# Attention plus gated dense branch: an ordering flag for VectorE at the last softmax sums, two PSUM banks for each first projection, and one load on another queue

## The chip, the core and the metric

The kernel runs on one NeuronCore of a Trainium2 chip. The core has TensorE (PE in the profile; its weight loads are PEld), VectorE (DVE), ScalarE (ACT), GpSimd (POOL) and SyncE (SP). DMAs are issued here from SP's queue and from ScalarE's queue. PSUM has eight banks, numbered 0 to 7 in this text; one bank holds 512 fp32 values in each of 128 partitions. The metric is the device time of one execution in microseconds; lower is better.

## The reference

Two branches are computed from the same input and mixed by a gate for each row. Branch A is attention with 32 heads of 20 columns each, over 2048 positions; branch B is a dense layer with a Mish activation.

```python
# x: (1, 2048, 640)   wqkv: (640, 1920)   wo: (640, 640)   w1: (640, 1536)   w2: (1536, 640)
g = sigmoid((x * gate_w).sum(-1, keepdims=True))

qkv = (x @ wqkv).reshape(B, S, 3, H, Dh).transpose(2, 0, 3, 1, 4)     # H = 32, Dh = 20
q, k, v = qkv[0], qkv[1], qkv[2]
p = softmax(einsum("bhqd,bhkd->bhqk", q, k) * Dh ** -0.5)
o = einsum("bhqk,bhkd->bhqd", p, v)
a = o.transpose(0, 2, 1, 3).reshape(B, S, D) @ wo

h = x @ w1 + b1
b = (h * tanh(softplus(h))) @ w2

out = g * a + (1 - g) * b
```

## The kernel before

**Tiling.** The 32 heads are taken four at a time, so there are 8 head groups p; the 2048 queries are taken in 4 chunks of 512. One pair (p, chunk) is a group, and there are 32 of them. In each, the scores of 16 key tiles are made for four heads, exponentiated (ScalarE on L1312, or a power-of-two approximation on VectorE on L473, L604 and GpSimd on L572) and multiplied with the values into the accumulator `acc`, which is PSUM bank 7 (L1355). A column of ones in the value tile gives the softmax sums beside the products.

**Order.** The order of the instructions on each engine is written out by hand: a small planner in the kernel's Python steps through a model of four engines and emits instructions as its model's engines come free. Each engine then runs its own stream in that order and waits on semaphores for the others. The planner takes VectorE's work from the list `dve_q`; an item carries a priority as its first field, and the lowest due time wins (`step_dve`). Items of priority 0 are the ones of `normalise`, below. Everything else on VectorE has priority 1 or more: evacuations of PSUM, powers, scalings.

**Start.** The first 512 rows of x come in four pieces (L317), two on each of the queues of SP and ScalarE. Then come the first columns of the K weights (`wf1`, `load_first(1)`, SP), the first columns of the Q weights (`wf0`, `load_first(0)`, ScalarE), `w_top` (48 further columns of the K weights, which go into the unused columns of the padded tile; L320, SP) and `wv0` (value weights of the first four heads; L321, ScalarE; the profile calls it `wv`). Behind them SP issues the rest of x and all other weights. The four pieces of x are transposed on TensorE (L1454) into `xT`. VectorE copies `wf1` and `w_top` into the padded tile `wkp` (L366, L1469) and `wf0` into `wqp` (L366). Then five products of 512 columns make the first K in one bank and five make the first Q in another (L1478). Of each result VectorE copies the first 256 columns (L1486) and ScalarE the last 256 (L1487), out of the same bank. The first scores (L1262) need both halves of both.

**End.** The last group is (p = 7, chunk 3). `normalise` handles it with four steps at priority 0, each put into the list when the one before is done: `a` transposes the accumulator (L1376), `b` takes the reciprocal of the sums and multiplies it by the gate (L1390, L1392), and `ends` scales and transposes the result in two halves (L1413, L1419) into `o_last[7]`. Heads groups 0 to 5 of the last chunk go through the output projection in eight chains of 16 products each (`wo_chain`, L637); each is evacuated on VectorE by L1064 into `R[LQ]` (in the tile `big`), for one 128-row block u and one half of the columns. After the planner's loop, 24 products fill all eight banks (`rest`, L1830): eight with `o_last[6]`, eight that add `R[LQ]` through the identity, eight with `o_last[7]`, always in the order u = 0 to 3, first half and second half. The banks by that order are 0, 1, 3, 4, 2, 5, 6, 7. Then the blocks are copied out and stored: blocks 0 and 1 on ScalarE, 128x640 each (L1845), both halves of block 2 and the first half of block 3 on VectorE (L1854), and the second half of block 3 on ScalarE (L1852). SP stores each block when it is ready (L1848, L1856).

Of the kernel before, what the change touches and what calls it, by code (L numbers as in the profile page):

```python
# [9 lines left out]
P = 128  # L10
# [54 lines left out]
def kernel(  # L65
# [12 lines left out]
    nc = tc.nc  # L78
    _, S, D = A_x.shape
    F = B_w1.shape[1]  # L80
    H = 32
    DH = D // H
    KT = D // P
    FT = F // P
    NS = S // P
    QC = 512
# [3 lines left out]
    HALF = D // 2  # L90
# [149 lines left out]
    xT = consts.tile([P, KT, S], BF16, tag="xT")  # L240
    VA = consts.tile([P, NS, H, DH + 1], BF16, tag="VA")
    wv0 = work.tile([P, KT, 4 * DH + 1], BF16, tag="bl1", name="wv0")
# [7 lines left out]
    wqp = consts.tile([P, KT, 4, 32], BF16, tag="wqp")  # L250
    wkp = consts.tile([P, KT, 4, 32], BF16, tag="wkp")
# [4 lines left out]
    allb = psum.tile([P, 8, QC], F32, tag="Sp", name="Sp")  # L256
# [3 lines left out]
    def bank_ap(tag, shape, dtype=F32):  # L260
        ap = allb[:, tag, :]
        if dtype != F32:
            ap = ap.bitcast(dtype)
        if len(shape) == 3:
            return ap[:, 0 : shape[1] * shape[2]].rearrange("p (a b) -> p a b", b=shape[2])
        return ap[:, 0 : shape[1]]
# [9 lines left out]
    wrows = A_wqkv.rearrange("(kt p) c -> p kt c", p=P)  # L276
# [8 lines left out]
    KTOP = D - KPAD  # L285
# [9 lines left out]
    w_top = work.tile([P, KT, KPAD], BF16, tag="bl0", name="w_top")  # L295

    def load_first(kind, eng):
        eng.dma_start(out=w_first[kind][:, :, :], in_=wrows[:, :, kind * D : kind * D + HF])
# [16 lines left out]
    for u in range(NU):  # L315
        eng = nc.sync if u % 2 == 0 else nc.scalar
        eng.dma_start(out=xs[0][:, u, :], in_=x2d[u * P : (u + 1) * P, :])  # L317
    load_first(1, nc.sync)
    load_first(0, nc.scalar)
    nc.sync.dma_start(out=w_top[:, :, :], in_=wrows[:, :, D + KTOP : 2 * D])  # L320
    nc.scalar.dma_start(out=wv0[:, :, 0 : 4 * DH], in_=wrows[:, :, 2 * D : 2 * D + 4 * DH])  # L321

    def load_x(c):
        nc.sync.dma_start(
# [6 lines left out]
        out=wv0[:, :, 4 * DH : 4 * DH + 1], in_=gate_w.rearrange("(kt p o) -> p kt o", p=P, o=1)  # L331
# [58 lines left out]
    act_q = deque()  # L390
    pool_q = []
    two_port = [0.0]
    seq = [0]
    free = {"PE": 0.0, "ACT": 0.0, "DVE": 0.0, "POOL": 0.0}
    mode = [None]
# [973 lines left out]
    def normalise(G, ready):  # L1369
        p, qc = groups[G]  # L1370
        i = G % 2
        st = {}

        def a(t):
            st["T1"] = work.tile([P, NS, 32], F32, tag=f"T1_{i}", name="T1")
            nc.vector.transpose(out=st["T1"][:, :, :].rearrange("p b r -> p (b r)"), in_=acc[:, :])  # L1376

        pr = 0 if G == NG - 1 else 2
        kept = qc == LQ and p >= NQ - NSB

        def a_done(t):
            acc_free[0] = t
            if G == NG - 1:
                dve(t, t, 140.0, b, prio=pr, done=lambda t: dve(t, t, 1300.0, ends, prio=pr))
                return
            dve(t, t, 140.0, b, prio=pr, done=lambda t: pool_q.insert(0, (t, 728.0, c, c_done, None)))

        def b(t):
            st["rec"] = work.tile([P, NS], F32, tag=f"rec{i}", name="rec")
            nc.vector.reciprocal(out=st["rec"][:, :], in_=st["T1"][:, :, DH])  # L1390
            if kept:
                nc.vector.tensor_tensor(  # L1392
                    out=st["rec"][:, :], in0=st["rec"][:, :], in1=g_rows[:, :], op=ALU.mult
                )

        def c(t):
            nc.gpsimd.tensor_tensor(  # L1397
                out=T2[i][:, :].rearrange("p (b r) -> p b r", r=32)[:, :, 0:DH],
                in0=st["T1"][:, :, 0:DH],
                in1=st["rec"][:, :].unsqueeze(2).to_broadcast([P, NS, DH]),  # L1400
                op=ALU.mult,
            )

        def d(t):
            st["O"] = work.tile([P, QC], BF16, tag=f"O{i}", name="O")
            nc.vector.transpose(out=st["O"][:, :], in_=T2[i][:, :])

        def ends(t):
            st["O"] = work.tile([P, QC], BF16, tag=f"O{i}", name="O")
            for h in range(2):  # L1410
                q = slice(h * QC // 2, (h + 1) * QC // 2)
                b_ = slice(h * NS // 2, (h + 1) * NS // 2)
                nc.vector.tensor_tensor(  # L1413
                    out=T2[i][:, q].rearrange("p (b r) -> p b r", r=32)[:, :, 0:DH],
                    in0=st["T1"][:, b_, 0:DH],
                    in1=st["rec"][:, b_].unsqueeze(2).to_broadcast([P, NS // 2, DH]),
                    op=ALU.mult,
                )
                nc.vector.transpose(out=st["O"][:, q], in_=T2[i][:, q])  # L1419
            o_last[p] = st["O"]  # L1420

        def c_done(t):
            if kept:
                dve(t, t, 640.0, d, prio=pr, done=lambda t: o_last.__setitem__(p, st["O"]))
                return
            rows = o_dram[qc * QC : (qc + 1) * QC, :].rearrange("(b i) f -> i b f", i=32)
            for k in range(4):
                r0 = (4 * p + k) * DH
                nc.sync.dma_start(
                    out=rows[:, :, r0 : r0 + DH],  # L1430
                    in_=T2[i][32 * k : 32 * k + 32, :].rearrange(
                        "p (b r) -> p b r", r=32
                    )[:, :, 0:DH],
                )
            last_p = NQ - 1 - (NSB if qc == LQ else 0)
            early = last_p * HF // P
            if p == last_p - 1 and qc != LQ:
                load_o(qc, range(early))
            elif p == last_p:
                load_o(qc, range(early, -(-(p + 1) * HF // P)))  # L1440
                o_ready[qc] = t + 9000.0
                if qc == LQ - 1:
                    load_o(LQ, range((NQ - NSB - 1) * HF // P))

        dve(0.0, ready, 640.0, a, prio=0, done=a_done)
# [24 lines left out]
        out=wkp[:, :, :, DH:32], in_=w_top[:, :, :].rearrange("p k (h d) -> p k h d", h=4)  # L1470
    )
    pad_copy(nc.vector, wqp, w_first[0][:, :, :])
    sb = [bank_ap(g, [P, QC]) for g in (6, 2)]
    kT[0] = kTb[0]
    qT[0] = qTb[0]
    for w, dst, k in ((wkp, kT[0][:, 0:QC], 0), (wqp, qT[0][:, :], 1)):
        for kt in range(KT):
            nc.tensor.matmul(  # L1478
                sb[k][:, :],
                lhsT=w[:, kt, :, :].rearrange("p h d -> p (h d)"),  # L1480
                rhs=xT[:, kt, 0:QC],
                start=(kt == 0),
                stop=(kt == KT - 1),
            )
        h_ = QC // 2
        nc.vector.tensor_copy(out=dst[:, 0:h_], in_=sb[k][:, 0:h_])  # L1486
        nc.scalar.copy(out=dst[:, h_:QC], in_=sb[k][:, h_:QC])  # L1487
    for p in range(NQ - NSB, NQ):
        tag = "wqp" if p < NQ - 1 else f"wo{p}"
        wo_pad[p] = consts.tile([P, D], BF16, tag=tag, name=f"wo{p}")  # L1490
# [249 lines left out]
    def step_dve(t):  # L1740
        best = None
        for it in dve_q:
            if it[1] <= t and (it[6] is None or it[6](t)):
                due = it[1] + (WAIT0, rule.WAIT1, rule.WAIT2, MWAIT)[it[0]]
                if it[0] == 3:
                    due = min(due, it[7] + WAIT3)
                if it[6] is not None and it[0] == 2 and cur["G"] > pv_G[0]:
                    due = min(due, it[1] + rule.WAITU)
                rank = (due, it[2])
                if best is None or rank < best[0]:  # L1750
                    best = (rank, it)
        if best is None:
            return None
        best = best[1]
        dve_q.remove(best)
        _, _, _, cost, fn, done, _, _ = best
        if rule.MERGE and best[2] in powers:
            o = beside(best, t)
            if o:
                dve_q.remove(o)  # L1760
                both(best, o, t)
                cost = 1134.0
                for x in (best, o):
                    x[5](t + cost + DVE_TAIL + SEM)
                return cost
        if best[0] == 2 and best[6] is not None:
            cost += max(free["POOL"] - t, 0.0)
            two_port[0] = t + cost
        fn(t)
        if done:  # L1770
            done(t + cost + DVE_TAIL + SEM)
        return cost
# [71 lines left out]
    for u in range(2):  # L1844
# [1 line left out]
            out=ots_[u][:, :].rearrange("p (a c) -> p a c", a=2), in_=(tx, ty)[u][:, 0:2, 0:HALF]  # L1846
        )
        nc.sync.dma_start(out=rows_[u], in_=ots_[u][:, :])  # L1848
    for u, half, eng in ((2, 0, 0), (2, 1, 0), (3, 0, 0), (3, 1, 1)):
        dst, src = ots_[u][:, half * HALF : (half + 1) * HALF], places[u][half][:, 0:HALF]  # L1850
        if eng:
            nc.scalar.copy(out=dst, in_=src)  # L1852
        else:
            nc.vector.tensor_copy(out=dst, in_=src)  # L1854
        if half:
            nc.sync.dma_start(out=rows_[u], in_=ots_[u][:, :])  # L1856
    if DEBUG:
        print("model end us", t / 1e3, "last exp", last_exp[0] / 1e3, {k: v / 1e3 for k, v in idle.items()}, "sets", sum(n_d), n_d, "heats", heats[0])

# [29 lines left out]
```

## Time and profile before

| | us |
|---|---|
| median of three runs | 722.08 |
| lowest and highest of them | 721.22, 722.51 |
| the profiled execution, its own time | 722.37 |
| span of the profiled execution, first to last instruction | 720.6 |
| TensorE busy in the span | 704.9 (98%) |
| ScalarE busy | 700.0 (97%) |
| VectorE busy | 631.6 (88%) |
| GpSimd busy | 418.1 (58%) |
| mean granted TensorE clock | 0.995 |

The span is 1.8 us shorter than the execution's time; that difference lies around the instructions. The profile lists the instructions of each engine with their lines in the kernel, the idle time before them and what ended it. "Chain of waits" stands for the view that follows the work that ended last back to what released it. Busy time of TensorE is modelled from pipelined products, so 98% is not 98% of its peak.

### The profile page before, as it was taken

What the parts mean: (1) busy time and instruction counts of PE and PEld (TensorE: products, weight loads), DVE (VectorE), ACT (ScalarE), POOL (GpSimd) and SP (SyncE); (2) the same over time, 40 slices, a digit from 0 to 9 for tenths busy, and PEclk for the clock granted to TensorE, in tenths of its full rate; (3) what the DMA queues carried; (4) which work ended last, traced back from release to release, by engine and by line L of the source; (5) the groups of instructions that cost most, each with busy time, mean ns of one, the idle gap of its engine ahead of it and who ended that gap; (6) DMA issues with size and microseconds to landing.
All of it is one profiled execution on the core that took longest, in us unless ns stands there. A gap on an engine that the chain in (4) does not pass through costs nothing.

```text
span 720.6 us, 24680 instructions
## 1 busy us (share of the span) xinstructions
PE 704.9 (98%) x10262; PEld 230.7 (32%) x10262; DVE 631.6 (88%) x1062; ACT 700.0 (97%) x726; POOL 418.1 (58%) x669
## 2 busy tenths in 40 slices
PE   7999999999999999999999999999989999999997
PEld 3433332222222333333333222222223333333333
DVE  4499998968868889999999998999998989999996
ACT  6899999999999999999999999999989999999996
POOL 2002864557868776877676687867964486762000
PEclk9999999999999999999999999999989999999999
DMA  9611122132322211111230223212211131131301
GB/s 249 180 24 33 31 47 52 34 69 57 80 43 51 50 29 17 23 32 28 46 92 25 46 51 84 65 43 43 60 20 30 33 68 27 31 63 15 61 20 47
DMA packets 123312, 37.86 MB, mean 53 GB/s; under 512 B 90880, under 2 KB 122640, under 8 KB 123200
## 3 DMA queue, kind: packets, MB, share of 16 engines
q1 hardware_dynamic: 121600, 35.76, 22.8%
q8 instruction: 80, 1.31, 0.8%
q10 hardware_dynamic: 1600, 0.53, 0.3%
q14 instruction: 32, 0.26, 0.2%
HBM read 22.29 MB, written 11.48 MB: 47 GB/s over the span
## 4 chain that ended last, share of the span: by engine, by line
PE 66%; ACT 25%; issue 5%; DVE 2%; DMA 1%; SPq 0%; POOL 0%; DVEq 0%; ACTq 0%
ACT E L1312 24%; PE Sp L1262 23%; PE Sp L637 21%; PE Sp L1355 21%; DVE T L473 1%; ACT big L924 1%; DMA w_top<-in_A_wqkv_dram 1%; PE Sp L1830 0%; DMA qT<-q_dram 0%; PE Sp L1478 0%; DVE T L604 0%; DMA q_dram<-st 0%; ACT L1312 0%; ACT L924 0%; DVE st L741 0%
## 5 line engine op out<-in xcount | busy, mean ns | idle before, releaser
L1312 ACT ACTIVATE E<-Sp 128x1024 bf16<-128x1024 f32 x710 | 668.8, 1079 | 6.8 <-PE Sp L1262 6.4
L572 POOL TENSOR_TENSOR T<-T,step_t 128x256 int32<-128x256 int32 x624 | 389.3, 659 | 108.0 <-PE Sp L1355 83.4
L473 DVE TENSOR_SCALAR T<-Sp 128x512 int16<-128x512 f32 (+1 forms) x595 | 391.9, 686 | 52.4 <-PE Sp L1262 46.3
L1262 PE MATMUL Sp<-qT,kT 32*128 32x512 bf16 x2048 | 288.3, 385 | 6.4 <-ACT E L1312 1.8
L1262 PEld LDWEIGHTS <-kT 32*128 32x128 bf16 x2048 | 74.2, 91 | 264.2 <-issue 260.0
L1355 PE MATMUL Sp<-E,VA 128*21 128x512 bf16 x1448 | 138.2, 383 | 0.0
L1397 POOL TENSOR_TENSOR T<-T,rec 128x320 bf16<-128x320 f32 x31 | 24.6, 792 | 164.9 <-DVE rec L1390 140.8
L604 DVE TENSOR_SCALAR T<-T 128x2048 int16<-128x2048 int16 x144 | 117.2, 819 | 1.4 <-PE Sp L1355 0.4
L1355 PE MATMUL Sp<-T,VD 128*21 128x512 bf16 x1200 | 113.5, 383 | 1.3 <-DVE T L604 1.3
L637 PE MATMUL Sp<-w_sb,big 128*32 128x320 bf16 x1536 | 79.4, 306 | 0.0
L637 PE MATMUL Sp<-xT,w1t 128*32 128x512 bf16 x960 | 76.6, 383 | 0.0
L1355 PEld LDWEIGHTS <-VA 128*21 128x21 bf16 x2048 | 45.2, 90 | 74.9 <-issue 67.3
L1355 PE MATMUL Sp<-T,VA 128*21 128x512 bf16 x600 | 58.2, 384 | 0.0
L637 PE MATMUL Sp<-xT,ws 128*32 128x512 bf16 x720 | 54.8, 382 | 0.2 <-DVE T L473 0.2
L637 PEld LDWEIGHTS <-big 128*32 128x32 bf16 x1536 | 34.8, 96 | 28.1 <-issue 18.5
L1355 PEld LDWEIGHTS <-VD 128*21 128x21 bf16 x1200 | 28.9, 90 | 37.5 <-issue 32.7
L891 DVE TENSOR_SCALAR big<-Sp,b1f 128x512 bf16<-128x512 f32 x48 | 35.6, 741 | 0.5 <-PE Sp L637 0.2
L637 PE MATMUL Sp<-wv,xT 128*32 128x81 bf16 (+2 forms) x960 | 33.0, 258 | 1.0 <-DVE T L473 1.0
L637 PE MATMUL Sp<-wo_sb,od 128*32 128x320 bf16 (+1 forms) x608 | 32.6, 302 | 0.0
L637 PEld LDWEIGHTS <-w1t 128*32 128x32 bf16 x960 | 19.6, 94 | 26.3 <-issue 21.2
L741 DVE CAST st<-Sp 128x512 bf16<-128x512 f32 x36 | 24.4, 681 | 3.8 <-PE Sp L637 3.3
L1376 DVE STREAM_TRANSPOSE T<-Sp 128x512 f32<-128x512 f32 x32 | 22.7, 709 | 2.1 <-PE Sp L1355 1.8
(74 smaller groups left out, 198.2 us busy)
## 6 DMA issues: line engine op xcount, KB each, us to landing
w1t<-in_B_w_dram SPq DMA_DIRECT2D x24, 320.0 KB
q_dram<-st SPq DMA_DIRECT2D x20, 128.0 KB
out_dram<-ot SPq DMA_DIRECT2D x16, 160.0 KB
qT<-q_dram SPq DMA_DIRECT2D x124, 20.0 KB
o_dram<-T SPq DMA_DIRECT2D x120, 20.0 KB
kT<-k_dram SPq DMA_DIRECT2D x28, 80.0 KB
k_dram<-st SPq DMA_DIRECT2D x16, 128.0 KB
big<-in_A_x_dram SPq DMA_DIRECT2D x3, 640.0 KB
```

The costliest lines, as they stand in the source:

```text
L473: nc.vector.tensor_scalar(out=dst.bitcast(I16), in0=src, scalar1=inv_sqrt_dh * LOG2E * 128.0, scalar2=127.0 * 128.0 + BETA, op0=ALU.mult, ...
L572: nc.gpsimd.tensor_tensor(out=tile_[:, :].bitcast(I32)[:, k * n : (k + 1) * n], in0=d["T"][:, :].bitcast(I32)[:, k * n : (k + 1) * n], in1 ...
L604: nc.vector.tensor_scalar(out=tile_[:, :].bitcast(I16), in0=d["T"][:, :].bitcast(I16), scalar1=float(SHIFT[i]), scalar2=None, op0=ALU.add,)
L637: nc.tensor.matmul(out_[k : k + 32], lhsT=lhsT[:, k : k + 32], rhs=rhs, tile_position=(0, k), **kw)
L741: nc.vector.tensor_copy(out=res["st"][:, :], in_=ps[:, :])
L891: nc.vector.tensor_scalar(out=big[:, slot.tag, (ft % 2) * QC : (ft % 2 + 1) * QC], in0=ps[:, :], scalar1=b1f[:, ft : ft + 1], scalar2=None ...
L924: lambda t: nc.scalar.activation(v, v, ACT.Mish), done,
L1262: nc.tensor.matmul(ps_cols, lhsT=kT[p][32 * t_ : 32 * t_ + 32, j * P : (j + 1) * P], rhs=qT[G][32 * t_ : 32 * t_ + 32, :], tile_position=( ...
L1312: nc.scalar.activation(E[:, x : x + n, :], ps, ACT.Exp, scale=inv_sqrt_dh,)
L1355: nc.tensor.matmul(acc[32 * t_ : 32 * t_ + DH + 1, :], lhsT=lhsT, rhs=rhs, start=(pv_done[G] == 0), stop=(pv_done[G] == pv_total[G] - 1), ...
L1376: nc.vector.transpose(out=st["T1"][:, :, :].rearrange("p b r -> p (b r)"), in_=acc[:, :])
L1397: nc.gpsimd.tensor_tensor(out=T2[i][:, :].rearrange("p (b r) -> p b r", r=32)[:, :, 0:DH], in0=st["T1"][:, :, 0:DH], in1=st["rec"][:, :].u ...
```

## The change

It has four parts.

1. A flag `closing` is set when the planner emits step `a` of the very last group, and cleared when it emits `ends`. While it is set, `step_dve` picks only items of priority 0.
2. The first K and the first Q are each computed in two banks, with ten products of 256 columns in place of five of 512: K in banks 1 and 4, Q in banks 5 and 0. VectorE copies out of the one bank and ScalarE out of the other.
3. `w_top` is issued on ScalarE's queue ahead of `wf0`, in place of third on SP's queue. `wv0` goes from ScalarE's queue to SP's.
4. At the end ScalarE copies the whole block 3 from banks 6 and 7 (128x640) after blocks 0 and 1, and VectorE copies only the two halves of block 2. The stores of blocks 2 and 3 stay on SP's queue in that order.

```diff
     load_first(1, nc.sync)
+    nc.scalar.dma_start(out=w_top[:, :, :], in_=wrows[:, :, D + KTOP : 2 * D])
     load_first(0, nc.scalar)
-    nc.sync.dma_start(out=w_top[:, :, :], in_=wrows[:, :, D + KTOP : 2 * D])
-    nc.scalar.dma_start(out=wv0[:, :, 0 : 4 * DH], in_=wrows[:, :, 2 * D : 2 * D + 4 * DH])
+    nc.sync.dma_start(out=wv0[:, :, 0 : 4 * DH], in_=wrows[:, :, 2 * D : 2 * D + 4 * DH])
...
         def a(t):
+            closing[0] = G == NG - 1
             st["T1"] = work.tile([P, NS, 32], F32, tag=f"T1_{i}", name="T1")
...
             o_last[p] = st["O"]
+            closing[0] = False
...
-    sb = [bank_ap(g, [P, QC]) for g in (6, 2)]
-    for w, dst, k in ((wkp, kT[0][:, 0:QC], 0), (wqp, qT[0][:, :], 1)):
+    h_ = QC // 2
+    for w, dst, two in ((wkp, kT[0], (1, 4)), (wqp, qT[0], (5, 0))):
         for kt in range(KT):
-            nc.tensor.matmul(
-                sb[k][:, :],
-                lhsT=w[:, kt, :, :].rearrange("p h d -> p (h d)"),
-                rhs=xT[:, kt, 0:QC],
...
-        h_ = QC // 2
-        nc.vector.tensor_copy(out=dst[:, 0:h_], in_=sb[k][:, 0:h_])
-        nc.scalar.copy(out=dst[:, h_:QC], in_=sb[k][:, h_:QC])
+            for h in range(2):
+                nc.tensor.matmul(
+                    allb[:, two[h], 0:h_],
+                    lhsT=w[:, kt, :, :].rearrange("p h d -> p (h d)"),
+                    rhs=xT[:, kt, h * h_ : (h + 1) * h_],
...
+        nc.vector.tensor_copy(out=dst[:, 0:h_], in_=allb[:, two[0], 0:h_])
+        nc.scalar.copy(out=dst[:, h_:QC], in_=allb[:, two[1], 0:h_])
...
-            if it[1] <= t and (it[6] is None or it[6](t)):
+            if it[1] <= t and (it[0] == 0 or not closing[0]) and (it[6] is None or it[6](t)):
...
-    for u, half, eng in ((2, 0, 0), (2, 1, 0), (3, 0, 0), (3, 1, 1)):
-        dst, src = ots_[u][:, half * HALF : (half + 1) * HALF], places[u][half][:, 0:HALF]
-        if eng:
-            nc.scalar.copy(out=dst, in_=src)
-        else:
-            nc.vector.tensor_copy(out=dst, in_=src)
-        if half:
-            nc.sync.dma_start(out=rows_[u], in_=ots_[u][:, :])
+    nc.scalar.copy(
+        out=ots_[3][:, :].rearrange("p (a c) -> p a c", a=2), in_=allb[:, 6:8, 0:HALF]
+    )
+    for half in range(2):
+        nc.vector.tensor_copy(
+            out=ots_[2][:, half * HALF : (half + 1) * HALF], in_=places[2][half][:, 0:HALF]
+        )
+    for u in (2, 3):
+        nc.sync.dma_start(out=rows_[u], in_=ots_[u][:, :])
```

More of the change, by code (lines that the diff above doesn't have):

```diff
@@ L392 @@
     two_port = [0.0]
+    closing = [False]
     seq = [0]
@@ L1472 @@
     pad_copy(nc.vector, wqp, w_first[0][:, :, :])
-    sb = [bank_ap(g, [P, QC]) for g in (6, 2)]
     kT[0] = kTb[0]
     qT[0] = qTb[0]
-    for w, dst, k in ((wkp, kT[0][:, 0:QC], 0), (wqp, qT[0][:, :], 1)):
+    h_ = QC // 2
+    for w, dst, two in ((wkp, kT[0], (1, 4)), (wqp, qT[0], (5, 0))):
         for kt in range(KT):
-            nc.tensor.matmul(
-                sb[k][:, :],
-                lhsT=w[:, kt, :, :].rearrange("p h d -> p (h d)"),
-                rhs=xT[:, kt, 0:QC],
-                start=(kt == 0),
-                stop=(kt == KT - 1),
-            )
-        h_ = QC // 2
-        nc.vector.tensor_copy(out=dst[:, 0:h_], in_=sb[k][:, 0:h_])
-        nc.scalar.copy(out=dst[:, h_:QC], in_=sb[k][:, h_:QC])
+            for h in range(2):
[3 more added lines that the diff above has]
+                    rhs=xT[:, kt, h * h_ : (h + 1) * h_],
+                    start=(kt == 0),
+                    stop=(kt == KT - 1),
+                )
+        nc.vector.tensor_copy(out=dst[:, 0:h_], in_=allb[:, two[0], 0:h_])
+        nc.scalar.copy(out=dst[:, h_:QC], in_=allb[:, two[1], 0:h_])
     for p in range(NQ - NSB, NQ):
@@ L1848 @@
         nc.sync.dma_start(out=rows_[u], in_=ots_[u][:, :])
-    for u, half, eng in ((2, 0, 0), (2, 1, 0), (3, 0, 0), (3, 1, 1)):
-        dst, src = ots_[u][:, half * HALF : (half + 1) * HALF], places[u][half][:, 0:HALF]
-        if eng:
-            nc.scalar.copy(out=dst, in_=src)
-        else:
-            nc.vector.tensor_copy(out=dst, in_=src)
-        if half:
-            nc.sync.dma_start(out=rows_[u], in_=ots_[u][:, :])
+    nc.scalar.copy(
[4 more added lines that the diff above has]
+            out=ots_[2][:, half * HALF : (half + 1) * HALF], in_=places[2][half][:, 0:HALF]
+        )
+    for u in (2, 3):
+        nc.sync.dma_start(out=rows_[u], in_=ots_[u][:, :])
     if DEBUG:
```

## The prediction

> **What bounds the kernel now.** I read the page first, then the chain of waits near both ends, then the timelines of 0 to 11 us and 712 to 721 us. On the page the chain that ended last runs through TensorE and ScalarE; VectorE and DMA have almost no share of it:
>
> ```profile
> span 720.6 us, 24680 instructions
> ...
> PE 66%; ACT 25%; issue 5%; DVE 2%; DMA 1%; SPq 0%; POOL 0%; DVEq 0%; ACTq 0%
> ```
>
> So a change around VectorE counts only where VectorE is what TensorE or ScalarE waits for. The chain of waits at the start (start us, length us, what) shows such a place:
>
> ```profile
> 2.12 4.46 DMA w_top<-in_A_wqkv_dram
> ...
> 6.60 0.23 DVE wkp L1469
> ...
> 6.88 2.35 PE Sp L1478 x10
> ...
> 9.31 0.44 DVE qT L1486
> ...
> 9.77 0.38 ACT qT L1487
> ...
> 10.20 0.45 PE Sp L1262 x4
> ```
>
> The reader should see two things: the load of `w_top` releases the K products, and ScalarE's half copy of Q starts when VectorE's has ended, so that the first scores wait for both in a row. The timeline of the end (start, length, engine, line, operation, operands) looks different:
>
> ```profile
> 712.36 0.70 DVE L1376 STREAM_TRANSPOSE T<-Sp 128x512 f32<-128x512 f32 x1
> ...
> 712.77 1.26 PE L1830 MATMUL Sp<-wo,O 128*128 128x320 bf16 x8
> 712.99 0.51 DVE L1064 SCALAR_TENSOR_TENSOR big<-Sp,g_t,xT 128x320 bf16<-128x320 f32 x1
> 713.42 0.24 DVE L1390 RECIPROCAL rec<-T 128x16 f32<-128x16 f32 x1
> ...
> 713.87 1.25 PE L1830 MATMUL Sp<-big,ident 128*128 128x320 bf16 x8
> ...
> 714.95 0.45 DVE L1419 STREAM_TRANSPOSE O<-T 128x256 bf16<-128x256 bf16 x1
> 714.95 1.25 PE L1830 MATMUL Sp<-wo,O 128*128 128x320 bf16 x8
> ...
> 717.17 0.94 SPq L1856 DMA_DIRECT2D out_dram<-ot  x2
> ```
>
> The 24 products of L1830 carry no idle time before them: 712.77, 713.87 and 714.95 are 8 x 0.136 apart. TensorE does not wait for VectorE here at all. And one piece of other work stands between the transpose of the last sums (L1376) and the reciprocal: the L1064 at 712.99, which evacuates the last block of the output projection.
>
> **The change part by part.** *The flag.* The only item it can hold back is that L1064, since nothing else of priority 1 stands between L1376 and the last L1419. It goes behind the last L1419. VectorE's own chain then starts earlier: the reciprocal follows L1376's end (712.36 + 0.70 = 713.07, and 0.03 more, as between L1390's end at 713.66 and the next operation at 713.69) at 713.10 in place of 713.42, 0.32 sooner. The last transpose ends at 715.40 - 0.32 = 715.08. This is worth nothing: the eight products that read it start at 714.95 because the sixteen before them last until then.
>
> What is late next: L1064 starts as the last transpose ends, 0.07 before its end as it now does behind L1376, so at 715.01, and ends at 715.51 (0.51 long). Who waits for it? Its bank must be empty before L1830 refills it. The first eight products go to banks 0, 1, 3, 4, 2, 5, 6, 7 at 0.136 each, so the sixth (bank 5) starts at 713.45, the seventh (bank 6) at 713.59. L1064 ends at 713.50, so its bank can be none of the first six, and bank 7 is the accumulator. It is bank 6. TensorE takes its products in order, so the seventh waits until about 715.51 + 0.05 (VectorE's `wkp` copy ends at 6.82, the weight load that waits for it starts at 6.87) = 715.56 instead of 713.59, and 17 more are queued behind it: one of the first eight, eight with the identity, eight with the last heads. All copies and stores wait for those. Cost: **+1.97**. Bounds: 1.9 if the wake-up is nothing, 2.05 if L1064 takes the 0.55 that four of its fellows take.
>
> *Block 3 copied by ScalarE alone.* Its two copies of 128x640 take 1.29 together, so the third ends about 0.65 after 716.77, at 717.42; today VectorE's half ends at 717.19. But SP's second store of L1856 begins only around 717.72, behind the one before it, so the 0.23 is covered by SP's queue. SP loses one wait between the two stores: 0 to -0.06, I take -0.02. End in all: **+1.95**.
>
> *`w_top` on ScalarE's queue.* It takes the place of `wf0`, so it is issued at 1.65 instead of 2.12. The trace's landing records put `wf0` at 6.06 and `w_top` at 6.58; with 60 KB in place of 100 KB it should land at about 6.05. L1469 then starts right behind L366 (5.80 + 0.26) at 6.08, 0.52 sooner, and K's products at 6.37. `wf0` becomes third on that queue, where the load landing last (`wv0`, 7.30) now stands; that is its upper bound, and 6.58 its lower one. Behind the waiting copy of `wf0` on VectorE stands only the copy of K, which is not ready before 7.4. In the bad case Q's weights are ready at 7.30 + 0.26 = 7.56 and Q starts at 7.61; in the good one it follows K's products at 6.37 + 1.09 = 7.46. Today it starts at 7.97. Gain 0.36 to 0.51, I take 0.43. `wv0` on SP's queue is used first at 12.93 (L637) and so is covered by 5 us; the x rows behind it (L647 at 10.53, landed 9.28) have 1.2 us of cover, and 40 KB more ahead of them cost about 0.1 us at the 350 GB/s of that stretch.
>
> *Two banks.* 256-column products are not in the trace. From 512 columns at 0.218 (five from 6.88 to 7.97) and 320 at 0.136, I estimate 0.109 each, ten for 1.09: no change. The second load of each weight tile (98 ns) hides under 0.109 as it does under the 0.136 of L1830; uncovered, ten loads would cost up to 0.98, and the nearest row speaks against it. ScalarE's copy starts with VectorE's at 9.31, not 9.77: 0.46, less a few ns per product, **0.43**. The copy of K was hidden under Q's products before.
>
> *How much of 0.86 arrives at the end.* Products, scores and exponentials are strings of semaphores and shift as one. Loads issued at fixed times do not. The tightest is the query tile of the second group; SP issues it behind the store it reads back, and that behind the big weight loads:
>
> ```profile
> 31.14 1.39 SPq L779 DMA_DIRECT2D qT<-q_dram  x4
> ```
>
> ```profile
> 34.49 0.39 PE L1262 MATMUL Sp<-qT,kT 32*128 32x512 bf16 x4
> ```
>
> The landing records put its last quarter at 33.78, with some of the 16 marks missing, and TensorE takes it at 34.49 without waiting. So 0.71 of the shift gets through, if nothing lands later; bounds 0 (it landed at 34.49) and 0.9 (the wait falls where ScalarE has work in stock). I take **-0.70**.
>
> Sum: -0.70 + 1.95 = **+1.25 us**. On the profiled execution, 722.37, that is 723.62; the median of the runs shown is 0.29 lower, so 722.08 + 1.25 = **723.3**.
>
> **Rivals.** *The start's gain is lost:* the query tile lands at 34.49, or the bubbles behind it swallow the rest. Then +1.95 alone: 724.0. For it: the missing marks; against: 33.78 on those present. 0.20.
>
> *The clock falls in the tail.* TensorE would now stand still from 713.73 to 715.56. The windows (stretch, its length, then busy us of PE, PEld, DVE, ACT, POOL, and the granted clock) show what thin work can do:
>
> ```profile
> 525.60:529.00 3.40, 2.25 (x15) 0.56 (x14) 3.40 (x6) 3.40 (x1) 0.12 (x1) 1.00 0.11 39
> ...
> 529.60:533.00 3.40, 3.18 (x21) 0.70 (x23) 3.40 (x7) 3.37 (x4) 2.90 (x5) 0.50 0.22 15
> ```
>
> After a stretch with TensorE two thirds busy, and no gap over 1.31 us, the clock was halved. If that happens in the new gap, 18 products take twice their 0.136: up to 2.45 more, 723.3 + 2.45 = 725.8. One such stretch in 720 us makes it rare: 0.06. The Trainium skill ("TensorE: Matmul & The Clock Gate", section "What's actually happening") asks for a whole idle window of about 3.4 us before the clock falls; by that, a gap of 1.8 us costs nothing. This trace disagrees: the clock fell after gaps of 1.31 us and less, so I keep the rival.
>
> *Not slower, bank 6 free:* the late L1064 empties a bank that L1830 refills later, or none. Then only the identity product of that block waits, the eighth of its eight, from 714.82 to 715.56: +0.74, which the start's 0.70 pays back: 722.1. It decides as soon as the seventh product starts by 713.7. For it: the bank is inferred from times 0.09 apart; 0.08.
>
> *VectorE is the bound at the end,* as the flag supposes: then 0.32 is gained there and 0.70 at the start, 721.1. It needs idle time before the last eight products, and there is none: 0.05.
>
> *The half-clock stretch at 529.6 is missing* in most runs afterwards: ScalarE waited 2.0 us for scores around it, so about 721.3. 0.06.
>
> **How the numbers follow.** The forecast has the remaining 0.55; its own range is 722.7 to 724.1 (start 0.4 to 0.9, end 1.9 to 2.05, and some 0.4 for the median, whose three runs span 1.3). What a measurement tells from no change is about 0.2%, 1.44 us: bounds 720.64 and 723.52. Slower: four tenths of the forecast (0.21), the lost gain (0.19), the clock (0.06): 0.46. Faster: tails of the last two rivals, 0.04. Within: 0.50. The range 722.0 to 724.7 leaves out the clock, most of the last two, and little else.
>
> **What would show it.** Right: L1064 behind the last L1419; an idle time of about 1.8 us on TensorE before the seventh L1830, ended by L1064; K's products at 6.4, the first scores near 9.3, the copies of Q side by side; the scores at 34.49 about 0.7 sooner; the distance from L1376 to the last instruction 2 us longer. Wrong: L1830 in one run without idle time, or a first score later than 9.8.

## The result, and the profile after

| | us |
|---|---|
| changed kernel, median of 18 runs | 724.45 |
| lowest and highest of them | 723.02, 728.84 |
| kernel before, median of 18 runs beside them | 722.36 |
| lowest and highest of them | 721.15, 723.53 |
| ratio, with its 95% interval | 1.0035 [1.0022, 1.0048] |
| the profiled execution of the changed kernel: time, span | 728.84, 727.1 |

The medians differ by 2.09 us, the means of the 18 by 2.59; the ratio, which lies near the means, puts the loss at 2.5 us. 1.25 us were forecast. Some of the executions are several microseconds longer than the rest: the ratio and the means count them, the medians hardly do, so both are given below. The profiled execution is the longest of the 18, 4.4 us over their median, so it shows more loss than the middle one. Its page:

```profile
span 727.1 us, 24700 instructions
...
PE 63%; ACT 25%; issue 5%; DMA 3%; SPq 2%; DVE 2%; POOL 0%; ACTq 0%
```

DMA and SP's queue have come into the chain, with 5% in place of 1%. The timeline of the end of the changed kernel (start, length, engine, line, operation, operands; idle time before and what ended it in brackets):

```profile
716.85 0.71 DVE L1378 STREAM_TRANSPOSE T<-Sp 128x512 f32<-128x512 f32 x1
...
717.26 0.99 PE L1833 MATMUL Sp<-wo,O 128*128 128x320 bf16 x6
717.59 0.25 DVE L1392 RECIPROCAL rec<-T 128x16 f32<-128x16 f32 x1
...
719.13 0.45 DVE L1421 STREAM_TRANSPOSE O<-T 128x256 bf16<-128x256 bf16 x1
719.50 0.51 DVE L1065 SCALAR_TENSOR_TENSOR big<-Sp,g_t,xT 128x320 bf16<-128x320 f32 x1
720.06 0.43 PE L1833 MATMUL Sp<-wo,O 128*128 128x320 bf16 x2 [1.82 <-DVE big L1065]
...
720.33 1.25 PE L1833 MATMUL Sp<-big,ident 128*128 128x320 bf16 x8
...
721.42 1.25 PE L1833 MATMUL Sp<-wo,O 128*128 128x320 bf16 x8
```

Six products run, then TensorE stands 1.82 us until the evacuation that the flag has sent behind VectorE's last transpose (L1421) is done. From the transpose of the last sums to the last instruction it is 10.21 us (727.06 - 716.85); before it was 8.23 (720.59 - 712.36).

The start of the changed kernel, in the same view:

```profile
6.18 0.22 DVE L1472 COPY wkp<-w_top 128x240 bf16<-128x240 bf16 x1
...
6.45 1.39 PE L1482 MATMUL Sp<-xT,wkp 128*128 128x256 bf16 x10
6.95 0.27 DVE L366 COPY wqp<-wf 128x400 bf16<-128x400 bf16 x1 [0.56 <-DMA wf<-in_A_wqkv_dram]
7.68 1.25 PE L1482 MATMUL Sp<-xT,wqp 128*128 128x256 bf16 x10
...
8.86 0.42 DVE L1489 CAST qT<-Sp 128x256 bf16<-128x256 f32 x1 [0.67 <-PE Sp L1482]
8.97 0.37 ACT L1490 CAST qT<-Sp 128x256 bf16<-128x256 f32 x1 [0.72 <-PE Sp L1482]
...
9.39 0.40 PE L1263 MATMUL Sp<-qT,kT 32*128 32x512 bf16 x4 [0.46 <-ACT qT L1490]
```

The copies of Q run side by side, and the first scores start at 9.39 in place of 10.20. The chain of waits shows where the 0.81 went (start, length, what):

```profile
19.43 10.29 DMA w_sb<-in_B_w_dram
...
30.13 3.92 DMA q_dram<-st
...
34.11 0.27 SPq L780
...
34.80 1.60 DMA qT<-q_dram
...
36.45 0.90 PE Sp L1263 x2
```

The chain of the first 36 us is now one of DMAs: the 2 MB of the second dense weights (`w_sb`), behind them the store of the second group's queries, behind it the load of the query tile that reads the store back. TensorE reaches the second group's scores at 36.45, about 2 us later than before, though it had begun 0.81 sooner. The same products, compared one by one with those before, are 0.81 us sooner up to 16 us, 0.56 sooner from 19 to 34 us, about 3 later at 36, 3.8 to 4.5 later from 43 us to the end of the attention, and 6.5 later in the last 18.

### The profile page after: what moved, and what is told of

Read it like the earlier page. It is cut to its first block, busy times and chain, and to the rows that moved or that the text cites. A ratio compares the mean times of both kernels' runs of the same rounds, so it can differ in the third digit from the quotient of the medians.

```text
span 727.1 us, 24700 instructions
## 1 busy us (share of the span) xinstructions
PE 710.1 (98%) x10272; PEld 233.3 (32%) x10272; DVE 631.5 (87%) x1061; ACT 700.8 (96%) x726; POOL 417.4 (57%) x669
## 4 chain that ended last, share of the span: by engine, by line
PE 63%; ACT 25%; issue 5%; DMA 3%; SPq 2%; DVE 2%; POOL 0%; ACTq 0%
ACT E L1313 23%; PE Sp L1263 23%; PE Sp L1356 20%; PE Sp L638 20%; DMA w_sb<-in_B_w_dram 1%; DMA q_dram<-st 1%; SPq L291 1%; ACT big L925 1%; SPq L304 1%; DMA big<-in_A_x_dram 1%; DVE T L474 0%; SPq L324 0%; SPq L337 0%; DVE T L605 0%; PE Sp L1833 0%
```

## The experiments

**One part at a time.** The flag alone on the kernel before:

```diff
+            closing[0] = G == NG - 1
...
+            if it[1] <= t and (it[0] == 0 or not closing[0]) and (it[6] is None or it[6](t)):
```

> The kernel before with the flag alone. Theory T (the flag's price at the end is fixed, the rest of the loss lies at the query tile of the second group): the distance from the last sums' transpose to the last instruction grows by 1.97 us, TensorE stands about 1.85 us before the seventh product of the last 24, first scores at 10.20 as before; time +2.0 us, ratio 1.0027. Rival F (the flag is covered and the whole loss comes from the start): ratio 1.000, no gap before the seventh product.

Measured: 723.88 against 721.81, ratio 1.0027 [1.0017, 1.0038]. Its end in the timeline:

```profile
712.30 0.99 PE L1833 MATMUL Sp<-wo,O 128*128 128x320 bf16 x6
...
714.54 0.51 DVE L1065 SCALAR_TENSOR_TENSOR big<-Sp,g_t,xT 128x320 bf16<-128x320 f32 x1
715.10 0.43 PE L1833 MATMUL Sp<-wo,O 128*128 128x320 bf16 x2 [1.82 <-DVE big L1065]
```

The same gap of 1.82 us, the seventh product behind it, and 10.20 us from the last sums' transpose to the end. So the flag's price at the end is 1.97 us (10.20 - 8.23), and it holds with the old start and the old copies too. The changed kernel without the flag:

```diff
-            closing[0] = G == NG - 1
```

> The changed kernel without the flag; the three other parts stay. Theory T: the end is as before the change (no gap in the last 24 products); the first scores stay at 9.39; what is gained there is lost again where TensorE meets the query tile of the second group, which lands at a time set by SP's loads: time between -0.7 and +0.5 us against the kernel before, ratio 0.999 to 1.0007. Rival F: it stays at the change's ratio, 1.0035.

Measured: 721.45 against 721.81, ratio 1.0001 [0.9992, 1.0009]; 8.22 us at the end. The median is 0.36 us lower than before, but the ratio shows no gain: the longer executions of this version take it back. Its first scores came at 9.86, because Q's weights arrived late and Q's products began only at 8.13. Its end also prices block 3 on ScalarE: 8.22 against 8.23, nothing. The loads alone and the banks alone:

```diff
+    nc.scalar.dma_start(out=w_top[:, :, :], in_=wrows[:, :, D + KTOP : 2 * D])
     load_first(0, nc.scalar)
-    nc.sync.dma_start(out=w_top[:, :, :], in_=wrows[:, :, D + KTOP : 2 * D])
-    nc.scalar.dma_start(out=wv0[:, :, 0 : 4 * DH], in_=wrows[:, :, 2 * D : 2 * D + 4 * DH])
+    nc.sync.dma_start(out=wv0[:, :, 0 : 4 * DH], in_=wrows[:, :, 2 * D : 2 * D + 4 * DH])
```

> The kernel before with the exchange of loads alone (w_top ahead of the first Q weights on ScalarE's queue, first value weights on SP's). Theory T: first scores 0.3 to 0.4 us sooner (about 9.85), query tile of the second group lands when SP's stream brings it, 0 to +0.3 us in the end: ratio 0.9995 to 1.0005. Rival Q (100 KB in place of 60 KB ahead of everything else on SP's queue is what makes the query tile late): the stores and loads around that tile come over 0.5 us later than before in every profile, ratio 1.001 to 1.003.

Measured: 721.67 against 721.81, ratio 1.0006 [0.9993, 1.0019]; lowest 720.6, highest 726.07. First scores at 10.03. The load of the query tile was issued at 31.12, before the change at 31.14: in this profile the 40 KB more on SP's queue don't make it late, and the rival, which asked for 0.5 us in every profile, falls.

```diff
-    sb = [bank_ap(g, [P, QC]) for g in (6, 2)]
...
+    for w, dst, two in ((wkp, kT[0], (1, 4)), (wqp, qT[0], (5, 0))):
...
```

> The kernel before with the first K and Q in two banks each, and nothing else. Theory T: first scores 0.43 us sooner (9.77), SP's stream untouched, the query tile of the second group at 33.8 in most executions, so most of the 0.43 arrives: -0.4 to 0 us, ratio 0.9995 to 1.0000. Rival Q: the same, -0.4 us, since SP's queue is as before. A rival for which twenty products with a weight load each are slower than ten: first scores no sooner than 10.1.

Measured: 721.78 against 721.81, ratio 1.0008 [0.9997, 1.0018]; highest 725.27. First scores at 9.78, so the 0.43 is there at the start; but the ratio lies above the expected 1.0000, and the gain does not arrive. The longest executions of the last two kernels are 4.4 us (loads) and 3.5 us (banks) over their median, though the banks alone leave SP's queue untouched. Neither was profiled.

**The load in front of the query tile.** The second dense weights are first read at 253 us. Their load was moved behind the third query tile, at 39 to 41 us, on four kernels (the fourth stands further below). The edit:

```diff
-    nc.sync.dma_start(out=w2_sb[:, :, :], in_=B_w2.rearrange("(ft p) c -> p ft c", p=P))
...
     events = [
+        (lambda t: next_q[0] >= 3, lambda t: load_w2()),
```

On the changed kernel without the flag:

> The changed kernel without the flag, and with the load of the second dense weights (2 MB) issued behind the third query tile (about 41 us) in place of ahead of the first key and query stores. Theory S (the start's gain is lost because the second group's query tile comes by SP's stream, behind that load): the query tile is issued by 28 us in place of 31, TensorE reaches the second group 0.5 to 0.8 us sooner than before and doesn't wait there; ratio 0.9985 to 0.9995, no execution over 1.5 us above the median. Rival B (the start's gain is swallowed by bubbles of TensorE and ScalarE in the first groups, whatever the loads): ratio 0.9995 to 1.0005 as without this edit, and the shift against before is gone by 34 us with no wait for a DMA.

Measured: 721.49 against 721.89, ratio 0.9994 [0.9985, 1.0003]; tile issued at 27.76, second group reached at 33.98 (34.49 before) without a wait, highest execution 0.9 us over the median. The profile is as theory S has it; the ratio alone, whose interval reaches 1.0003, would not part it from rival B. On the kernel before:

> The kernel before with the load of the second dense weights moved in the same way and nothing else. Theory S: the query tile had about 0.7 us of cover in most executions, so little is gained: 0 to -0.4 us, ratio 0.9995 to 1.0000, and the spread of the executions shrinks. Rival B: no change. If the load was itself what set the time of the start, it gains as much as the same edit on the changed start.

Measured: 721.90 against 721.89, ratio 0.9997 [0.9989, 1.0006]. With the old start the load in front costs nothing that shows. On the changed kernel with its flag:

> The changed kernel with its flag and its order of the last products, and the late load of the second dense weights. Theory T+S: the flag's price alone less a part of the start's gain: ratio 1.0018 to 1.0026, no execution more than 1.5 us above the median; no wait for the query tile in the profile. If the late query tile had no part in the change's loss, it stays with the changed kernel.

Measured: 724.02 against 722.55, ratio 1.0015 [1.0007, 1.0024], a little under the expected range; highest execution 0.29 us over the median. SP's queue in its timeline:

```profile
23.90 1.27 SPq L744 DMA_DIRECT2D q_dram<-st  x1
...
26.94 1.39 SPq L779 DMA_DIRECT2D qT<-q_dram  x4
...
39.28 0.41 SPq L1532 DMA_DIRECT2D w_sb<-in_B_w_dram  x1
```

The tile comes 7 us sooner than in the changed kernel (34.11). By the ratio 1.1 us are lost (0.0015 x 722.55), so of the flag's 1.97 about 0.9 us are paid back here, with an uncertainty of some 0.6 us: with the tile early, part of the new start's gain does arrive. Beside it on the same chip ran the changed kernel once more, and the one without the flag:

> The changed kernel once more, beside the others of this set on the same chip. Theory T+S: the flag's 1.97 us and a start whose gain is lost on the median: ratio 1.0025 to 1.0035. If the flag and the new start together cost more than the sum of the two alone, over 1.0035 here while the one without the flag stays at 1.0000.

> The changed kernel without the flag once more, beside it. Theory T+S: 1.97 us faster than the changed kernel, ratio 0.999 to 1.0005, with single executions 2 us and more above the median when the query tile of the second group is late.

Measured: 724.72 and 722.02 against 722.55, ratios 1.0026 [1.0017, 1.0036] and 1.0003 [0.9990, 1.0016]. Without the flag the median is 0.53 us below that of the kernel before, and the ratio again shows no gain. Three of the twelve executions without the flag were 2.6 to 4.3 us over their median; the profiled one, 726.35, shows TensorE waiting 2.42 us for the query tile:

```profile
36.62 0.63 PE L1263 MATMUL Sp<-qT,kT 32*128 32x512 bf16 x2 [2.42 <-DMA qT<-q_dram]
```

Then the tile was delayed in the kernel before, by issuing the load twice, the second time for nothing.

```diff
     nc.sync.dma_start(out=w2_sb[:, :, :], in_=B_w2.rearrange("(ft p) c -> p ft c", p=P))
+    nc.sync.dma_start(out=w2_sb[:, :, :], in_=B_w2.rearrange("(ft p) c -> p ft c", p=P))
```

> The kernel before, unchanged start and end, with the load of the second dense weights issued twice in a row (the second time for nothing), so that SP's stream brings the query tile of the second group some 6 us later. Theory S: TensorE and ScalarE stand still before the second group for 5 to 7 us; the granted clock is halved for a stretch behind it; time +5 to +10 us. Rival: the tile has so much cover, or so much other work stands ready, that the time moves by less than 2 us; then a late tile can't be what made single executions of the change 3 to 5 us longer.

Measured: 734.36 against 722.55 (two runs), ratio 1.016 [1.014, 1.0181]. Who waited, from 30 to 50 us, in total, times and longest:

```profile
ACT E L1313 <- PE Sp L1263: 10.4, 3, 9.6
PE Sp L1263 <- DMA qT<-q_dram: 8.1, 1, 8.1
```

It is more than expected because SP issues the second load only when the first has landed (at 28.52, after 8.8 us of waiting for it); the tile was issued at 40.66, 9.5 us later than before. The tile has no cover, that is time between its landing and its use, beyond a fraction of a microsecond: 9.5 us of delay cost 11.8 us, with a clock of 0.50 for 10.2 us behind the wait.

**Another order of the last products.** The flag stays; those of the 24 products that need bank 6 or the late block come last.

```diff
-    for p in (*list(wo_pad)[:-1], None):
-        for u in range(NU):
...
+    blocks = [(u, half) for u in range(NU) for half in range(2)]
+    early_, late_ = blocks[:6], blocks[6:]
+    for u, half in early_ + late_[1:]:
+        rest(u, half, NQ - NSB)
+    for u, half in early_:
+        rest(u, half, None)
+    for u, half in early_:
+        rest(u, half, NQ - 1)
+    rest(*late_[0], NQ - NSB)
+    for p in (None, NQ - 1):
+        for u, half in late_:
+            rest(u, half, p)
```

> The changed kernel with its flag; the 24 last products in another order: those that need bank 6 or the last evacuated block come last. Theory T (the flag costs 1.97 us only through what is queued behind bank 6): no gap of 1.85 us on TensorE, the last product starts 0.1 to 0.4 us after its place before the change, and the price of the flag falls to between -0.3 and +0.4 us: 1.5 to 2.3 us faster than the changed kernel, ratio to the kernel before 0.9995 to 1.0010. Rival: the late evacuation is the last work itself, whatever the order: the price stays over 1 us, ratio over 1.0015.

Measured: 721.76 against 721.89, ratio 0.9998 [0.9989, 1.0007]. Its end:

```profile
711.71 0.70 DVE L1378 STREAM_TRANSPOSE T<-Sp 128x512 f32<-128x512 f32 x1
...
713.89 1.32 PE L1833 MATMUL Sp<-wo,O 128*128 128x320 bf16 x7
...
714.36 0.51 DVE L1065 SCALAR_TENSOR_TENSOR big<-Sp,g_t,xT 128x320 bf16<-128x320 f32 x1
...
715.33 0.43 PE L1833 MATMUL Sp<-wo,O 128*128 128x320 bf16 x2
```

The late evacuation is unchanged; only what stands behind it is. From the last sums' transpose to the end it is now 7.82 us, 2.39 less than in the changed kernel and 0.41 less than before. So the price was the queue behind bank 6, not the evacuation. The ratio hardly shows the better end; the new start still has the load in front of its query tile here. With both edits:

> Both: the changed kernel with its flag, the 24 last products in the other order and the late load of the second dense weights. Theories S and T together: ratio 0.9980 to 0.9995, the fastest of all. If only T holds: as with the other order alone. If only S holds: over 1.0010.

Measured: 721.17 against 721.89, ratio 0.9990 [0.9982, 0.9999]. This version beats the changed kernel, and the kernel before by 0.7 us, which is just clear of the noise.

## Why the prediction was half right

**The end: right in every step.** What the flag holds back is one L1064; bank 6; six products, then the wait; the seventh 1.97 later. Forecast +1.97, measured 10.20 - 8.23 = 1.97 with the flag alone; the gap was forecast as 1.8 and is 1.82. (The upper bound of that term, with 0.55 for L1064, comes to about 2.02 by its own figures and not to 2.05.) ScalarE's copy of block 3 was forecast at -0.02 and is within 0.01 of nothing.

**The first scores: right, and a little small.** From Q's first product to the first scores it took 2.23 us with one bank (the five profiles with the old banks) and 1.71 to 1.73 with two: 0.51, where 0.43 was taken. With the loads exchanged K's products start at 6.45 (forecast 6.37) and Q's at 7.68, just outside the two cases of 7.46 and 7.61: ten products of 256 columns took 1.23 there, where 1.09 was estimated (1.10 and 1.14 in two of the experiments). The first scores came at 9.39, forecast "near 9.3". They spread, though: 9.1 to 9.9 in the eight profiles of the whole new start, 10.1 to 10.5 in the four of the old one. And the 7.30 taken as the latest landing of Q's weights is no bound: in the first profile without the flag their copy waited for the load until 7.81.

**The step that failed: "So 0.71 of the shift gets through, if nothing lands later".** The term of -0.70 measured as nothing: without the flag, where it should have stood alone, the ratios are 1.0001 and 1.0003, or +0.1 and +0.2 us; with the flag, what is left over the 1.97 is +0.6 and -0.1 us. The query tile's landing, 33.78, was read from one execution and used as a fixed time. It isn't one. (The lower bound of 0, stated beside the term, was also dropped from the forecast's own range, which goes by 0.4 to 0.9.) The tile hangs on SP's queue behind the 2 MB load: one of SP's stores of K waits until that load has landed, and the store and the load of the second group's queries stand behind it. SP's wait, before the change and after:

```profile
SPq L707 <- DMA w_sb<-in_B_w_dram: 4.7, 1, 4.7
...
SPq L708 <- DMA w_sb<-in_B_w_dram: 3.3, 1, 3.3
```

In the nine profiles with one such load in its old place SP issued the tile at 30.61 (without the flag), 30.91 (flag alone), 31.12 (loads alone), 31.14 (before), 31.48 (other order), 31.69 (banks alone), 34.01 and 34.11 (the changed kernel, twice) and 34.28 (without the flag, again). The old start reaches the tile's place at 34.4 to 34.8 us and is mostly covered; the whole new one reaches it at 33.7 to 34.2 and uses up the cover (with the other order, where the tile was issued at 31.48, TensorE already waited 0.16 us). From there on the loss can be larger than the gain ever was. The changed kernel's waits from 30 to 46 us:

```profile
ACT E L1313 <- PE Sp L1263: 4.3, 3, 3.5
...
PE Sp L1263 <- DMA qT<-q_dram: 2.1, 1, 2.1
```

and its stretches around it (stretch, its length, busy us of PE, PEld, DVE, ACT, POOL, granted clock):

```profile
33.00:36.30 3.30, 1.32 (x16) 0.31 (x15) 0.29 (x1) 2.44 (x3) 0.00 (x0) 1.00 0.09 27
36.30:39.70 3.40, 3.25 (x20) 0.47 (x19) 1.29 (x2) 0.74 (x1) 0.00 (x0) 0.50 0.13 31
```

A wait of 2.1 us, and behind it a clock of 0.50 for 6.8 us, together moved the products behind them by 4.7 us. Counted over all sets: with the sooner start (whole or in part) and the load in its old place, 9 of 85 executions were over 2 us above their kernel's median; with the old start 1 of 116; with the load moved 0 of 44, of which 33 have the sooner start. Three of the nine were profiled, and all three show the wait. With the load moved, 0.9, 0.4 and 0.3 us of the new start arrived by the ratios (with the flag, without it, and with the other order, whose end alone gains 0.41). In each pair of kernels the moved load brought 0.5 to 0.8 us; each difference alone is not clear of noise, but all three have one sign, and on the old start the same move brought 0.2.

**The rivals.** "The start's gain is lost" is what happened; it gave 724.0, and 724.45 was measured, beside a kernel before whose median was itself 0.28 higher than the one the forecast started from. That the two lie so close is partly luck. Its reason was half of it: not a tile landing always at 34.49, but one whose landing spreads over 3 to 4 us, and costs most executions little and a few of them several microseconds. "The clock falls in the tail" did not occur: all products behind the gap of 1.82 us run at 0.136 apart. It occurred at the other gap, where I had not put it. "Bank 6 free" and "VectorE is the bound" fall with the gap. "The half-clock stretch at 529.6 is missing" falls too: it is there in all 14 profiles.

**What stays open.** Why the tile is about 3 us late in three profiles, all of them with the sooner start. They don't have one reason. In the changed kernel the store of the queries is issued 1.1 us later than before (30.13, 29.04), behind a 2 MB load that landed later by as much; but it then takes 3.9 us where 2.1 is usual. While its packets moved, from 31 to 33 us, a packet of the queue that the profile calls instruction was on one of the DMA engines for 1.7 us (5.4% of sixteen engines in 2 us):

```profile
q1 hardware_dynamic: 227, 0.17, 28.2%
q8 instruction: 1, 0.02, 5.4%
```

Before, that packet came at 32.1, after the store. The other profile of the changed kernel shows the same meeting (packet at 31.17 for 1.6 us, store 3.8). That the packet holds up the store is a guess from these records; it was not tried apart. In the third late profile, without the flag, the delay came earlier: the 2 MB load was itself issued at 21.47, where before it was 18.85, because SP took longer over the loads ahead of it, and the store and the tile follow from there:

```profile
21.47 0.53 SPq L343 DMA_DIRECT2D w_sb<-in_B_w_dram  x1
...
31.70 0.84 SPq L745 DMA_DIRECT2D q_dram<-st  x1
...
34.28 1.39 SPq L780 DMA_DIRECT2D qT<-q_dram  x4
```

Open too is an idle time of TensorE at 18 to 19 us, put to "issue", in which most profiles with both parts lose 0.25 to 0.5 us of the start's gain. Last, the stretch at half clock near 530 us lasted 6.8 us in eight profiles and 10.2 us in six. In the six, the products behind it stood 0.6 to 0.7 us later, against those before, than the products ahead of it. The changed kernel is one of the six, and so are the three versions with the new start and the moved load, so in their profiles a good part of the start's gain is lost there. What decides its length is not known.

## What to carry to other kernels

Ask of a held-back instruction which buffer it empties and who is queued behind that buffer, not how long it takes: half a microsecond of evacuation cost two because 18 products in order stood behind its bank, and a change of their order took the price away. A gain at the start counts only up to the first load that doesn't move with it; that load's cover, read from one profile, is one draw from a spread, and a kernel that used to be just late enough can become one that waits. Before shortening a start, put the large loads that nobody needs yet behind the small ones that the next stage reads. And compare means as well as medians: here the medians without the flag stood 0.4 to 0.5 us below the kernel before and the ratios did not, for a few long executions.

## What the runs showed of the hardware

Waits of 2 us and more of TensorE for the query tile were followed by half clock. In the changed kernel TensorE was busy for 1.32 of the 3.30 us before 36.3, and from there the granted clock was 0.50. In all four profiles in which TensorE waited for the tile 2.0 us or longer (2.01, 2.13, 2.42 and 8.1) the clock fell to 0.50 between 36 and 39 us; in the other ten it stayed at full there. Before the change, near 529.6, TensorE had been busy for two thirds of the stretch ahead. The gap of 1.82 us in the end, followed by dense work, did nothing: the products behind it ran at 0.136 apart. The Trainium skill ("TensorE: Matmul & The Clock Gate", section "What's actually happening") asks for an idle window of about 3.4 us; these rows disagree as far as a whole idle window is meant: a partly idle one was enough. The stretches at half clock that both began and ended among the work of a profile were 3.4, 6.8 or 10.2 us long, multiples of that window, as the page's window of fixed length would have it.
